# One excursion per pair of heads instead of two, the relu divided between two engines, and a new load order in a fused attention and feed-forward kernel

## The chip, the cores and the metric

The kernel runs on one core of a Trainium2 chip. The metric is the device time of the program in microseconds (us), the median of the runs. Runs of one kernel agree within about 0.3%. Profiled executions have a *span*, from the first to the last instruction, which is about 2 us shorter than the time. All numbers below are of one core; every profiled run that is compared had the state "fast".

Engines are named as in the profile: PE is the matmul engine (TensorE), PEld its weight loads, DVE is VectorE, ACT is ScalarE, POOL is GpSimd, SP the SyncE queue, which issues transposes by DMA and the output.

## The reference

Attention with a squared relu in place of softmax, then a feed-forward network with layer normalisation and a residual:

```python
scores = q @ k.T / sqrt(64)                      # q, k, v: 8 batches, 12 heads, 448 x 64
attn   = maximum(scores, 0)**2 / 448
x      = (attn @ v)  # heads side by side: 8 x 448 x 768
mu, var = mean(x), var(x)                        # over the 768
xn  = (x - mu) / sqrt(var + 1e-6) * g
out = x + maximum(xn @ w1, 0) @ w2               # w1: 768 x 3072, w2: 3072 x 768
```

Inputs and output are fp32; the kernel multiplies in bf16.

## The kernel before

The work is cut into 48 pairs of heads (8 batches, 6 pairs each). A pair has four score tiles; each is two matmuls of 64 rows (one per head) into one *score slot*, of which there are two. A relu and a square make the attention tile from it, and eight matmuls of 64 columns multiply it by v ("AV", one pair later).

```python
ps_sc = tile_pool(name="ps_sc", bufs=2, space=PSUM)   # two score slots
ps_f  = tile_pool(name="ps_f",  bufs=2, space=PSUM)   # feed-forward outputs
ps_m  = tile_pool(name="ps_m",  bufs=2, space=PSUM)   # AV, means, transposes

def att_QK(i, t):
    at = attn_pool.tile([SP, 2, S], bf16, tag="attn")
    sc = ps_sc.tile([P, 2, 512], fp32, tag="sc")
    for hh in range(2):
        nc.tensor.matmul(sc[:SP, hh, :S], ...)         # L209, 64 rows of the array
    nc.scalar.activation(at, sc[:SP, :, :S], Act.Relu) # L211, ScalarE reads the slot
    nc.vector.tensor_mul(at, at, at)                   # L212, square

def step_a(i): att_QK(i, 0); att_QK(i, 1)
def step_b(i):
    att_QK(i, 2); att_QK(i, 3); att_AV(i - 1)
    if ...: att_T(i + 3)                    # DMA transpose of q, k on the SP queue
```

The feed-forward matmuls use the whole array: `ps` blocks of 6 matmuls of 448 columns (first layer, L290) and `o_ps` blocks of 24 matmuls of 384 columns (second layer, L306). Between parts of such blocks the kernel pulls in the steps of the list above. I call each leaving of the full-array matmuls for the 64-row and 64-column ones an *excursion*. There are two per pair: 4 score matmuls, and 4 score plus 8 AV matmuls.

The feed-forward network runs for two batches at a time: first layer of one batch, first layer of the other, second layer of both. During the first layer of the second batch six DMA transposes (`ffn_x`, SP queue) turn x into rows, and DVE takes the statistics of these rows, which the output needs:

```python
if bb == 1 and ni < K1:
    items.append((0.0, lambda u=u, ki=ni: ffn_x(u, ki)))
if bb == 1 and ni >= K2 - MU:                                # from block 17 of 24
    items.append((0.0, lambda u=u, m=ni - (K2 - MU): ffn_stats(u, m)))
```

Batches 0 and 1 (pairs 0 to 11) have their q and k transposed on PE; from batch 2 (pair 12) on, the SP queue transposes them by DMA. Loads with a cast stand on one queue, and batch 2 stands behind w2:

```python
for c in range(W2C):       # W2C = 4
    load_w2(c)
load_paired(2)
```

Of the kernel before, what the change touches and what calls it, by code (L numbers as in the profile page):

```python
# [11 lines left out]
def kernel(  # L12
# [10 lines left out]
    nc = tc.nc  # L23
    P = 128
# [16 lines left out]
    U = 2  # L41
    UT = U * S
    MU = UT // P
    assert SP * NJ == S and MU * P == UT
    c2 = (1.0 / D) / S

# [38 lines left out]
    def alloc_batch(b):  # L85
        v_sb = v_pool.tile([SP, H, NJ * D], bf16, tag="v_sb")
        if b == 1:
            half = h1[:SP, :, S:S + NJ * D]
            qkv[b] = (half[:, :H, :], half[:, H:2 * H, :], v_sb)
            return  # L90
        q_sb = io_pool.tile([SP, H, NJ * D], bf16, tag="q_sb")
        k_sb = io_pool.tile([SP, H, NJ * D], bf16, tag="k_sb")
        qkv[b] = (q_sb, k_sb, v_sb)
# [19 lines left out]
                    by_pair[:, a, :, x, :],  # L113
                    src[b, 2 * a + x].rearrange("(p j) d -> p j d", j=NJ))

    def load_paired(b):
        alloc_batch(b)
        for a in range(NPAIR):
            load_pair(b, a)
            if a == 1:  # L120
                load_heads(b, [("v", 0, H)])
# [78 lines left out]
        qkT[i] = qkT_t  # L200
        nc.vector.tensor_copy(qkT[i], tp[0])  # L201

    def att_QK(i, t):
        at = attn_pool.tile([SP, 2, S], bf16, tag="attn")
        attn[i, t] = at
        sc = ps_sc.tile([P, 2, 512], fp32, tag="sc")
        for hh in range(2):
            r = slice(hh * D, (hh + 1) * D)
            nc.tensor.matmul(sc[:SP, hh, :S], qkT[i][r, 1, t * SP:(t + 1) * SP], qkT[i][r, 0, :],  # L209
                             start=True, stop=True)  # L210
        nc.scalar.activation(at, sc[:SP, :, :S], Act.Relu)  # L211
        nc.vector.tensor_mul(at, at, at)  # L212

    av = {}
    xs = {}
# [1 line left out]
    def xT_of(b, ki):  # L217
        return xT[b // U][:, ki, (b % U) * S:(b % U + 1) * S]

    def att_AV(i, half=None):  # L220
        b, pr = divmod(i, NPAIR)
        v_sb = qkv[b][2]
        if pr == 0 and half != 1:
            if b % U == 0:
                xT_t = xT_pool.tile([P, K1, UT], bf16, tag="xT")
                xT[b // U] = xT_t
            xs_t = xs_pool.tile([P, S], bf16, tag="xs")
            xs[b] = xs_t
        if half != 1:
            av_ps = ps_m.tile([P, S], fp32, tag="m")  # L230
            av[0] = av_ps
        ps = av[0]
        for t in range(NJ) if half is None else range(half * 2, half * 2 + 2):
            for hh in range(2):
                nc.tensor.matmul(  # L235
                    ps[hh * D:(hh + 1) * D, :],
                    v_sb[:, 2 * pr + hh, t * D:(t + 1) * D],
                    attn[i, t][:, hh, :],
                    start=(t == 0), stop=(t == NJ - 1))
        if half == 0:  # L240
            return
        nc.vector.tensor_scalar(xT_of(b, pr), ps, c2, None, op0=Alu.mult)  # L242
        if pr == 1:
            nc.vector.tensor_add(xs[b], xT_of(b, 0), xT_of(b, 1))
        elif 1 < pr < NPAIR - 1:
            nc.vector.tensor_add(xs[b], xs[b], xT_of(b, pr))  # L246

    xc = {}

    def center(b):  # L250
        mean_ps = ps_m.tile([P, S], fp32, tag="m")
        nc.tensor.matmul(mean_ps, ones, xs[b], start=True, stop=False)  # L252
        nc.tensor.matmul(mean_ps, ones, xT_of(b, K1 - 1), start=False, stop=True)  # L253
        xc_t = xc_pool.tile([P, K1, S], bf16, tag="xc")
        xc[b] = xc_t
        for ki in range(K1):
            nc.vector.tensor_sub(xc_t[:, ki, :], xT_of(b, ki), mean_ps)  # L257
# [38 lines left out]
    def ffn_2(u, m, j, part, parts):  # L296
        hd = d_model // 2
        if part == 0:
            if j == 0:
                o_t = o_pool.tile([P, d_model], fp32, tag="o")  # L300
                o_sb[0] = o_t
            o_ps = ps_f.tile([P, hd], fp32, tag="f")
            o_sb[1] = o_ps
        n = K2 // parts
        for ki in range(part * n, (part + 1) * n):
            nc.tensor.matmul(o_sb[1], h1[:, ki, m * P:(m + 1) * P], w2[:, ki, j * hd:(j + 1) * hd],  # L306
                             start=(ki == 0), stop=(ki == K2 - 1))
        if part == parts - 1:
            nc.vector.scalar_tensor_tensor(  # L309
                o_sb[0][:, j * hd:(j + 1) * hd], o_sb[1], rstd[u][:, m:m + 1],  # L310
                x_tok[u][:, m, j * hd:(j + 1) * hd], op0=Alu.mult, op1=Alu.add)
            if j == 1:
                c0 = m * P
                while c0 < (m + 1) * P:
                    g0 = c0 // SP
                    c1 = min((m + 1) * P, (g0 + 1) * SP)
                    bb, jj = divmod(g0, NJ)
                    nc.sync.dma_start(
                        out_tok[u * U + bb, c0 - g0 * SP:c1 - g0 * SP, jj, :],
                        o_sb[0][c0 - m * P:c1 - m * P, :])  # L320
                    c0 = c1


    def warm_up(n):
        w_ps = ps_f.tile([P, 256], fp32, tag="f")
        for _ in range(n):
            nc.tensor.matmul(w_ps, ones, warm, start=True, stop=True)  # L327
# [5 lines left out]
    def step_a(i):  # L333
        att_QK(i, 0)
        att_QK(i, 1)

    def step_b(i):
        att_QK(i, 2)
        att_QK(i, 3)
        if i > 0:  # L340
            att_AV(i - 1)
        if i + 2 < PE_T * NPAIR:
            att_T(i + 2)
        if PE_T * NPAIR <= i + 3 < NP_ALL:
            att_T(i + 3)
        b, r = divmod(i + 4, NPAIR)
        if r == 0 and PE_T < b < B:
            load_paired(b)

    def step_fine(i):  # L350
        att_QK(i, 0)
        if 0 < i < NPAIR - 1:
            att_T(i + 1)
        elif i > 0:
            warm_up(4)
        att_QK(i, 1)
        if i == 0:
            att_T(1)
            warm_up(1)
        else:  # L360
            att_AV(i - 1, 0)
        att_QK(i, 2)
        if i == 0:
            warm_up(4)
        else:
            att_AV(i - 1, 1)
        att_QK(i, 3)
        warm_up(4)

    def first_end():  # L370
        att_AV(NPAIR - 1, 0)
        att_T(NPAIR, evac=False)
        warm_up(4)
        att_AV(NPAIR - 1, 1)
        warm_up(8)
        center(0)
        att_T_out(NPAIR)

    for i in range(NP_ALL):
        if i < NPAIR:  # L380
            att.append(lambda i=i: step_fine(i))
        elif i == NPAIR:
            att.append(first_end)
            done_at.append(len(att))
            att.append(lambda i=i: (step_a(i), att_T(i + 1)))
            att.append(lambda i=i: (att_QK(i, 2), att_QK(i, 3), att_T(i + 2)))
        else:
            att.append(lambda i=i: step_a(i))
            att.append(lambda i=i: step_b(i))
            if i % NPAIR == 0:  # L390
                att.append(lambda b=i // NPAIR - 1: center(b))
                done_at.append(len(att))
# [4 lines left out]
    def steps_of(b):  # L397
        return done_at[b]

    NU = B // U  # L400
    segs = []
    CPN = K2 // NCH
    for u in range(NU):
        for bb in range(U):
            items = []
            for ni in range(K2):
                if bb == 0 and u == 0 and ni % CPN == 0 and ni // CPN + 1 < NCH:
                    c = ni // CPN + 1
                    items.append((0.0, lambda c=c: prep_w1(c, nc.vector, K1 // 2 if c < 3 else 0, K1)))
                if bb == 1 and ni < K1:  # L410
                    items.append((0.0, lambda u=u, ki=ni: ffn_x(u, ki)))
                if bb == 1 and ni >= K2 - MU:
                    items.append((0.0, lambda u=u, m=ni - (K2 - MU): ffn_stats(u, m)))
                items.append((1.12, lambda u=u, bb=bb, ni=ni: ffn_1(u, bb, ni)))
            segs.append((u * U + bb, items))
        items = []
        for m in range(MU):
            for j in range(2):
                for part in range(4):
                    items.append((0.96, lambda u=u, m=m, j=j, p=part: ffn_2(u, m, j, p, 4)))  # L420
                    if m + j + part == 0:
                        items.append((0.0, lambda u=u: ffn_stats(u, MU)))
        segs.append((u * U + U - 1, items))
# [6 lines left out]
    def pull():  # L430
        nonlocal ai
        att[ai]()
        ai += 1

    with tc.manual_schedule(engines=set(ENGINES)):
# [15 lines left out]
        warm_up(5)  # L451
        while ai < steps_of(0):
            pull()
        for c in range(W2C):
            load_w2(c)
        load_paired(2)

        pace = [(0.0, steps_of(0))]
        t = 0.0
# [51 lines left out]
```

## Time and profile before

| | before |
|---|---|
| time, median (lowest to highest) | 585.82 us (585.38 to 586.06) |
| span of the profiled run | 583.8 us |
| PE busy | 563.6 us, 97% |
| longest wait of PE | 8.93 us, at 72.5 us |

The page of the kernel before: the busy time of PE and ACT and DVE, then PE in 40 slices of the span (tenths), then the granted clock.

```profile
PE 563.6 (97%) x3542; PEld 287.3 (49%) x3542; DVE 263.6 (45%) x505; ACT 266.7 (46%) x392; POOL 143.3 (25%) x188
...
PE   8989949999999999999999999999999999999996
...
PEclk9999969999999999999999999999999999999999
```

PE is busy for 80% or more of every slice but the sixth (73 to 88 us) and the last, and in the sixth the clock falls too. That slice in the timeline of PE of the kernel before (start, duration, line, operation, shapes, count; in brackets the idle time before it and its releaser), and then one ordinary pair of excursions:

```profile
71.16 1.31 PE L290 MATMUL ps<-xc_t,w_112 128*128 128x448 bf16 x6
81.40 1.00 PE L209 MATMUL sc<-qkT_t 64*112 64x448 bf16 x4 [8.93 <-DMA qkT_t<-k_sb]
...
299.61 0.59 PE L209 MATMUL sc<-qkT_t 64*112 64x448 bf16 x4
300.13 0.95 PE L235 MATMUL av_ps<-at,v_sb 112*64 112x448 bf16 x8
301.01 4.07 PE L306 MATMUL o_ps<-w_113,h_114 128*128 128x384 bf16 x24
305.01 0.59 PE L209 MATMUL sc<-qkT_t 64*112 64x448 bf16 x4
305.53 5.05 PE L306 MATMUL o_ps<-w_113,h_114 128*128 128x384 bf16 x30
```

First reading: at 72.47 us PE stops for 8.93 us, because the transposed q and k of pair 12 are not there. Second reading, from starts: an excursion with AV takes 301.01 - 299.61 = 1.40 us, one without 0.52 us, a block of 24 matmuls 4.00 us. PE does not wait in either excursion.

Why pair 12 is late, in the timeline of the SP queue of the kernel before (the issue of transposes; the duration is the issue, not the landing):

```profile
72.27 1.29 SPq L177 DMA_TRANSPOSE qkT_t<-q_sb  x1
...
88.57 7.79 SPq L267 DMA_TRANSPOSE x_t<-xT_t  x5
...
101.60 1.25 SPq L267 DMA_TRANSPOSE x_t<-xT_t  x1
```

The transpose of pair 12 could be issued at 72.27 us only, when q had arrived behind w2. The first five transposes of x were issued from 88.57 us and the sixth at 101.60 us. In this kernel the first statistics came at 117.34 us.

What the stop did to the clock, in the windows of the kernel before (stretch, length, busy time of the engines; the value after POOL is the granted clock):

```profile
72.50:76.00 3.50, 0.00 (x0) 0.00 (x0) 1.11 (x3) 0.54 (x1) 3.50 (x6) 1.00 1.07 97
76.00:81.40 5.40, 0.00 (x0) 0.00 (x0) 0.00 (x0) 0.00 (x0) 2.30 (x4) 0.50 1.49 167
81.40:86.20 4.80, 4.80 (x18) 1.61 (x20) 1.25 (x2) 3.12 (x4) 3.94 (x6) 0.50 2.31 145
```

The clock fell to one half 3.5 us after the stop, and came back 4.8 us after PE resumed, at 86.2 us. The work in those 4.8 us cost about 2.2 us more than elsewhere. The Trainium skill ("TensorE: Matmul & The Clock Gate", Part 1) describes this: half clock after an idle window of about 3.4 us, full clock after a sustained busy one. The trace agrees for this fall (3.5 us). The windows also show a step: this stretch at half clock lasted 10.24 us (75.97 to 86.21 us), which is three times 3.41 us. With the 8.93 us of the stop the hole cost some 11.1 us.

Last, three groups of instructions of the kernel before (line, engine, operation, out and in, shapes, count, then busy us and mean ns of one, then idle time ahead):

```profile
L211 ACT ACTIVATE at<-sc 112x896 bf16<-112x896 f32 x192 | 165.0, 915 | 138.1 <-PE sc L209 137.6
...
L212 DVE TENSOR_TENSOR at<-at 112x896 bf16<-112x896 bf16 x192 | 120.2, 632 | 184.2 <-ACT at L211 184.2
...
L242 DVE TENSOR_SCALAR xT_t<-av_ps 128x448 bf16<-128x448 f32 x48 | 29.6, 617 | 3.6 <-PE av_ps L235 3.6
```

All relus are on ScalarE, 915 ns each; VectorE does the squares. The third line is how fast VectorE reads fp32 from PSUM: 617 ns for 448 columns.

### The profile page before, as it was taken

The page shows a single profiled execution, that of the slowest core. Times are in us where ns is not written, and L with a number is a line of the kernel's source. Part 1 is how long each engine was busy: PE and PEld are TensorE (multiplying, and loading weights), DVE is VectorE, ACT ScalarE, POOL GpSimd, SP SyncE. Part 2 cuts the span into 40 slices and gives each one's busy share as a digit, 9 for nine tenths or more (in the row PEclk, how much of TensorE's full clock was granted, in tenths as well). Part 3 has the DMA queues.
Part 4 walks back from the last instruction along what each step waited for, and adds up shares of the span by engine and source line. Part 5 has one row for each costly group of instructions (what it writes and reads, how often), then busy time and mean ns, then how long its engine had stood idle before and what let it go on. Part 6 is the DMA issues. An engine that isn't in the chain of part 4 may idle for free.

```text
span 583.8 us, 8969 instructions
## 1 busy us (share of the span) xinstructions
PE 563.6 (97%) x3542; PEld 287.3 (49%) x3542; DVE 263.6 (45%) x505; ACT 266.7 (46%) x392; POOL 143.3 (25%) x188
## 2 busy tenths in 40 slices
PE   8989949999999999999999999999999999999996
PEld 5444414445555444445555544445555544556663
DVE  4977814284544334375444424256454334401111
ACT  6937825672233576663232475664313364440000
POOL 7793170163006500074003610074000000000000
PEclk9999969999999999999999999999999999999999
DMA  9999999299218933599125954299223141000121
GB/s 181 201 205 210 195 145 129 38 116 96 71 44 105 154 36 58 78 111 104 44 71 66 169 54 80 47 95 112 54 58 73 47 71 33 0 2 28 55 54 55
DMA packets 153242, 51.79 MB, mean 89 GB/s; under 512 B 125808, under 2 KB 149616, under 8 KB 153200
## 3 DMA queue, kind: packets, MB, share of 16 engines
q0 software_dynamic: 90144, 25.50, 45.3%
q1 hardware_dynamic: 62576, 25.25, 22.0%
q8 instruction: 28, 0.46, 0.3%
q10 hardware_dynamic: 480, 0.46, 0.3%
q14 instruction: 14, 0.11, 0.1%
HBM read 51.91 MB, written 11.01 MB: 108 GB/s over the span
## 4 chain that ended last, share of the span: by engine, by line
PE 90%; DVE 5%; DMA 2%; ACT 1%; issue 0%; SPq 0%; ACTq 0%
PE o_ps L306 38%; PE ps L290 37%; PE sc L209 7%; PE av_ps L235 6%; DVE at L212 2%; ACT at L211 1%; DMA qkT_t<-k_sb 1%; DVE xc_t L257 1%; DMA h_114<-in_q_dram 1%; DVE qkT_t L201 1%; DVE xT_t L242 0%; DVE xs_t L246 0%; PE tp_ps L190 0%; PE mean_ps L253 0%; PE mean_ps L252 0%
## 5 line engine op out<-in xcount | busy, mean ns | idle before, releaser
L290 PE MATMUL ps<-xc_t,w_112 128*128 128x448 bf16 x1152 | 230.1, 354 | 1.8 <-DVE xc_t L257 1.8
L211 ACT ACTIVATE at<-sc 112x896 bf16<-112x896 f32 x192 | 165.0, 915 | 138.1 <-PE sc L209 137.6
L306 PE MATMUL o_ps<-w_113,h_114 128*128 128x384 bf16 x1344 | 225.6, 326 | 0.0
L212 DVE TENSOR_TENSOR at<-at 112x896 bf16<-112x896 bf16 x192 | 120.2, 632 | 184.2 <-ACT at L211 184.2
L306 PEld LDWEIGHTS <-h_114 128*128 128x128 bf16 x1344 | 128.6, 98 | 95.0 <-issue 12.2
L290 PEld LDWEIGHTS <-w_112 128*128 128x128 bf16 x1152 | 108.7, 98 | 115.6 <-issue 18.8
L292 ACT ACTIVATE h_114<-ps 128x448 bf16<-128x448 f32 x192 | 104.6, 545 | 110.6 <-PE ps L290 110.3
L112 POOL DMA_DIRECT2D q_sb<-in_q_dram x72 | 50.3, 703 | 213.1 <-DMA qkT_t<-q_sb 114.8
L309 DVE SCALAR_TENSOR_TENSOR o_t<-o_ps,rstd_t,x_t 128x384 f32<-128x384 f32 x56 | 34.5, 616 | 82.1 <-PE o_ps L306 82.1
L209 PE MATMUL sc<-qkT_t 64*112 64x448 bf16 x384 | 59.8, 378 | 10.3 <-DMA qkT_t<-k_sb 8.9
L112 POOL DMA_DIRECT2D k_sb<-in_k_dram x72 | 50.2, 701 | 38.8 <-DMA v_sb<-in_v_dram 26.2
L235 PE MATMUL av_ps<-at,v_sb 112*64 112x448 bf16 x384 | 47.3, 361 | 1.0 <-DVE at L212 0.6
L209 PEld LDWEIGHTS <-qkT_t 64*112 64x112 bf16 x384 | 18.4, 126 | 46.4 <-issue 34.3
L257 DVE TENSOR_TENSOR xc_t<-xT_t,mean_ps 128x448 bf16<-128x448 bf16 x48 | 26.2, 614 | 16.2 <-PE mean_ps L253 16.2
L242 DVE TENSOR_SCALAR xT_t<-av_ps 128x448 bf16<-128x448 f32 x48 | 29.6, 617 | 3.6 <-PE av_ps L235 3.6
L235 PEld LDWEIGHTS <-v_sb 112*64 112x64 bf16 x384 | 17.6, 109 | 24.7 <-issue 18.3
L159 POOL TENSOR_SCALAR w_112<-w_112,g_sb 128x512 bf16<-128x512 bf16 x12 | 20.8, 1744 | 1.3 <-DMA w_112<-in_moe_w_ch_dram 1.3
L284 DVE BATCH_NORM_STATS2 stats<-x_t 128x6 f32<-128x384 bf16 x28 | 15.2, 542 | 0.0
L283 DVE BATCH_NORM_STATS2 stats<-x_t 128x6 f32<-128x384 bf16 x28 | 14.6, 523 | 0.0
L327 PE MATMUL w_ps<-w_113,ones 128*128 128x256 bf16 x70 | 11.4, 304 | 1.2 <-DVE w_113 L77 1.2
L279 DVE RECIPROCAL rstd_t<-rstd_t 128x7 f32<-128x7 f32 x4 | 0.8, 201 | 22.5 <-ACT rstd_t L278 22.5
L246 DVE TENSOR_TENSOR xs_t<-xs_t,xT_t 128x448 bf16<-128x448 bf16 x24 | 10.0, 416 | 0.8
(36 smaller groups left out, 81.0 us busy)
## 6 DMA issues: line engine op xcount, KB each, us to landing
v_sb<-in_v_dram POOLq DMA_DIRECT2D x7, 672.0 KB, 10.0
w_112<-in_moe_w_ch_dram POOLq DMA_DIRECT2D x6, 768.0 KB, 25.8
w_113<-in_moe_w_ch_dram POOLq DMA_DIRECT2D x4, 1152.0 KB, 19.1
q_sb<-in_q_dram POOLq DMA_DIRECT2D x72, 56.0 KB, 4.1
k_sb<-in_k_dram POOLq DMA_DIRECT2D x72, 56.0 KB, 4.1
out_dram<-o_t SPq DMA_DIRECT2D x8, 336.0 KB, 2.8
out_dram<-o_t SPq DMA_DIRECT2D x8, 288.0 KB, 2.6
out_dram<-o_t SPq DMA_DIRECT2D x8, 240.0 KB, 2.6
```

The lines of the kernel that those rows point to most:

```text
L112: nc.gpsimd.dma_start(by_pair[:, a, :, x, :], src[b, 2 * a + x].rearrange("(p j) d -> p j d", j=NJ))
L159: eng.tensor_scalar(w, w, g_sb[:, ki:ki + 1], None, op0=Alu.mult)
L209: nc.tensor.matmul(sc[:SP, hh, :S], qkT[i][r, 1, t * SP:(t + 1) * SP], qkT[i][r, 0, :], start=True, stop=True)
L211: nc.scalar.activation(at, sc[:SP, :, :S], Act.Relu)
L212: nc.vector.tensor_mul(at, at, at)
L235: nc.tensor.matmul(ps[hh * D:(hh + 1) * D, :], v_sb[:, 2 * pr + hh, t * D:(t + 1) * D], attn[i, t][:, hh, :], start=(t == 0), stop=(t == N ...
L242: nc.vector.tensor_scalar(xT_of(b, pr), ps, c2, None, op0=Alu.mult)
L257: nc.vector.tensor_sub(xc_t[:, ki, :], xT_of(b, ki), mean_ps)
L290: nc.tensor.matmul(ps, w1[:, ki, ni * P:(ni + 1) * P], xc[u * U + bb][:, ki, :], start=(ki == 0), stop=(ki == K1 - 1))
L292: nc.scalar.activation(h1[:, ni, bb * S:(bb + 1) * S], ps, Act.Relu)
L306: nc.tensor.matmul(o_sb[1], h1[:, ki, m * P:(m + 1) * P], w2[:, ki, j * hd:(j + 1) * hd], start=(ki == 0), stop=(ki == K2 - 1))
L309: nc.vector.scalar_tensor_tensor(o_sb[0][:, j * hd:(j + 1) * hd], o_sb[1], rstd[u][:, m:m + 1], x_tok[u][:, m, j * hd:(j + 1) * hd], op0=A ...
```

## The change

The intent: fewer changes between the full array and its parts. From batch 2 on a pair makes one excursion: two score slots, AV of the pair behind, two score slots. As slots three and four reuse slots one and two at once, the relus are divided between VectorE and ScalarE, so that the slots come free sooner; the four squares come after. Besides, the first two pairs of batch 2 are loaded ahead of w2, the statistics start at block 10 and take every second block, the mean of batch 0 is summed pair by pair on PE, and the last output tile is written in halves.

```diff
-    def load_paired(b):
-        alloc_batch(b)
-        for a in range(NPAIR):
+    def load_paired(b, a0=0, a1=NPAIR):
+        if a0 == 0:
+            alloc_batch(b)
+        for a in range(a0, a1):
...
-        nc.scalar.activation(at, sc[:SP, :, :S], Act.Relu)
-        nc.vector.tensor_mul(at, at, at)
+        if relu_by is nc.vector:
+            nc.vector.tensor_scalar(at, sc[:SP, :, :S], 0.0, None, op0=Alu.max)
+        else:
+            nc.scalar.activation(at, sc[:SP, :, :S], Act.Relu)
+        if relu_by is None:
+            att_square(i, t)
...
+    def step_one(i):
+        att_QK(i, 0, relu_by=nc.vector)
+        att_QK(i, 1, relu_by=nc.scalar)
+        att_AV(i - 1)
+        att_QK(i, 2, relu_by=nc.vector)
+        att_QK(i, 3, relu_by=nc.scalar)
+        for t in range(NJ):
+            att_square(i, t)
+        next_T(i)
...
-            att.append(lambda i=i: step_a(i))
-            att.append(lambda i=i: step_b(i))
+            if i < PE_T * NPAIR:
+                att.append(lambda i=i: step_a(i))
+                att.append(lambda i=i: step_b(i))
+            else:
+                att.append(lambda i=i: step_one(i))
...
-                if bb == 1 and ni >= K2 - MU:
-                    items.append((0.0, lambda u=u, m=ni - (K2 - MU): ffn_stats(u, m)))
+                m = (ni - (K2 - 2 * MU)) // 2
+                if bb == 1 and m >= 0 and ni % 2 == 0:
+                    items.append((0.0, lambda u=u, m=m: ffn_stats(u, m)))
...
+        load_paired(2, 0, 2)
         for c in range(W2C):
             load_w2(c)
-        load_paired(2)
+        load_paired(2, 2)
```

(`att_square` holds the square; `next_T`, the end of the old `step_b`, issues the transposes of pair i + 3.)

More of the change, by code (lines that the diff above doesn't have):

```diff
@@ L43 @@
     MU = UT // P
+    NU = B // U
     assert SP * NJ == S and MU * P == UT
@@ L201, in att_T_out, with att_QK @@
         nc.vector.tensor_copy(qkT[i], tp[0])
-    def att_QK(i, t):
+    def att_QK(i, t, relu_by=None):
         at = attn_pool.tile([SP, 2, S], bf16, tag="attn")
@@ L210, in att_QK, with att_square @@
                              start=True, stop=True)
-        nc.scalar.activation(at, sc[:SP, :, :S], Act.Relu)
-        nc.vector.tensor_mul(at, at, at)
+        if relu_by is nc.vector:
[4 more added lines that the diff above has]
+            att_square(i, t)
+    def att_square(i, t):
+        nc.vector.tensor_mul(attn[i, t], attn[i, t], attn[i, t])
     av = {}
@@ L226, in att_AV @@
                 xT[b // U] = xT_t
-            xs_t = xs_pool.tile([P, S], bf16, tag="xs")
-            xs[b] = xs_t
+            if b > 0:
+                xs_t = xs_pool.tile([P, S], bf16, tag="xs")
+                xs[b] = xs_t
         if half != 1:
@@ L242, in att_AV @@
         nc.vector.tensor_scalar(xT_of(b, pr), ps, c2, None, op0=Alu.mult)
+        if b == 0:
+            return
         if pr == 1:
@@ L248, with mean_part @@
     xc = {}
-    def center(b):
-        mean_ps = ps_m.tile([P, S], fp32, tag="m")
-        nc.tensor.matmul(mean_ps, ones, xs[b], start=True, stop=False)
+    mean0 = {}
+    def mean_part(ki):
+        if ki == 0:
+            mean0_ps = ps_f.tile([P, S], fp32, tag="f")
+            mean0[0] = mean0_ps
+        nc.tensor.matmul(mean0[0], ones, xT_of(0, ki), start=(ki == 0), stop=(ki == K1 - 1))
+    def center(b):
+        if b == 0:
+            mean_ps = mean0[0]
+        else:
+            mean_ps = ps_m.tile([P, S], fp32, tag="m")
+            nc.tensor.matmul(mean_ps, ones, xs[b], start=True, stop=False)
         nc.tensor.matmul(mean_ps, ones, xT_of(b, K1 - 1), start=False, stop=True)
@@ L311, in ffn_2 @@
                 x_tok[u][:, m, j * hd:(j + 1) * hd], op0=Alu.mult, op1=Alu.add)
-            if j == 1:
+            last = u == NU - 1 and m == MU - 1
+            if j == 1 or last:
+                d0, d1 = (j * hd, (j + 1) * hd) if last else (0, d_model)
                 c0 = m * P
@@ L318, in ffn_2 @@
                     nc.sync.dma_start(
-                        out_tok[u * U + bb, c0 - g0 * SP:c1 - g0 * SP, jj, :],
-                        o_sb[0][c0 - m * P:c1 - m * P, :])
+                        out_tok[u * U + bb, c0 - g0 * SP:c1 - g0 * SP, jj, d0:d1],
+                        o_sb[0][c0 - m * P:c1 - m * P, d0:d1])
                     c0 = c1
@@ L343, in step_b, with next_T @@
             att_T(i + 2)
+        next_T(i)
+    def next_T(i):
         if PE_T * NPAIR <= i + 3 < NP_ALL:
@@ L348, in step_b @@
             load_paired(b)
+    def step_one(i):
[6 more added lines that the diff above has]
+            att_square(i, t)
+        next_T(i)
     def step_fine(i):
@@ L367, in step_fine @@
         att_QK(i, 3)
-        warm_up(4)
+        if i > 1:
+            mean_part(i - 2)
+            warm_up(2)
+        else:
+            warm_up(4)
     def first_end():
@@ L372, in first_end @@
         att_T(NPAIR, evac=False)
-        warm_up(4)
+        mean_part(NPAIR - 2)
+        warm_up(2)
         att_AV(NPAIR - 1, 1)
@@ L387 @@
         else:
-            att.append(lambda i=i: step_a(i))
-            att.append(lambda i=i: step_b(i))
+            if i < PE_T * NPAIR:
+                att.append(lambda i=i: step_a(i))
+                att.append(lambda i=i: step_b(i))
+            else:
+                att.append(lambda i=i: step_one(i))
             if i % NPAIR == 0:
@@ L398, in steps_of @@
         return done_at[b]
-    NU = B // U
     segs = []
```

## The prediction

> **What bounds the kernel now.** TensorE: the page gives PE 563.6 of 583.8 us (97%), and the chain of waits lies 90% on PE. The table of waits shows one real hole: 8.93 us (72.5 to 81.4) for the DMA transpose of batch 2's first pair, whose loads sit behind four w2 loads on the same queue (its waits on w_113 last until 71.8). The granted clock then fell to 0.5: in the timeline the next two blocks take 3.28 and 2.09 us against 1.76 and 1.40 elsewhere. Together about 11.1 us.
>
> **What the change does, costed.**
>
> 1. *One excursion per pair.* The timeline of PE shows 24 full-array matmuls of 384 columns in 4.00 us and 30 in 4.98: 163 ns each plus about 0.09 us per block. The Trainium skill ("TensorEngine Tiling (Array Packing)", Key Properties) says a change of tiling mode drains the array; the trace agrees in kind. One block less for each of 36 pairs: -3.2 us.
>
> 2. *A wait for score slots.* There are two score buffers. Slot two now starts behind 4 score and 8 AV matmuls, 1.40 us after the excursion's start (299.61 to 301.01). The first score is readable at +0.44 us (when ScalarE starts today). VectorE took 617 ns for 448 fp32 columns of PSUM; the skill ("VectorE: DVE Perf Modes", Mode 2×_2P) says two-port reading is SBUF only, so 896 should take about 1.08 us (estimate: 617 less 150 fixed, doubled). It ends at 1.52, so TensorE waits about 0.18 us in 30 excursions. In five excursions of the first second-layer stage an output eviction (616 ns) stands just ahead on VectorE: about 0.4 us. Together +7 us. VectorE rises by about 75 us, ScalarE falls by 66; neither becomes the bound.
>
> 3. *Pairs 0, 1 and v of batch 2 before w2.* The hole goes, with its cold clock: -11 us.
>
> 4. *But statistics seven blocks earlier.* In the first two batches they now stand on VectorE ahead of the relu of pair 14, and need all six transposes of x. Those queue on SyncE behind the transposes of pairs 14 and 15, which still wait for loads behind w2. DMA is saturated from 40 to 90 us in both orders, so these loads should land near 82 us (83.3 before). Then 5 us of transposes, 8 of x (88.6 to 96.4 today), 2.6 for pair 16, the last x transpose and 2.9 to landing: about 101.5. Statistics and relu end near 103.6; TensorE would want slot two near 95.8. I expect a new hole of 4 to 8 us there, perhaps 2 us of cold clock: most of step 3 is given back.
>
> 5. Small: first mean without sums (-1), batch 1's mean subtracted late behind four squares (+0.8), last output in two pieces (-0.3).
>
> Sum, with the hole at the small end for doubt: 584 us, 577 to 590. Chances: faster 8%, within 2% 90%, slower 2%.
>
> **What would show it.** The hole at 72 us gone; a PE wait on VectorE's relu for the score tile in nearly every excursion, 5 to 9 us in total; one PE wait of 4 to 8 us near 96 to 104 us, with VectorE's statistics waiting on the x transposes; relu on VectorE near 1.08 us; blocks of 42 to 48 matmuls between excursions.
>
> **What would make it wrong.** If w2 loads run faster in the new order, or the x transposes land before about 95 us, hole 4 vanishes: near 577. If VectorE reads PSUM faster than estimated, step 2 vanishes and 5 to 7 us more go, giving over 2%. If VectorE falls behind in the stages with statistics (about 10.3 us of work in a 10.5 us period), step 2 grows.

## The result

| | before | after |
|---|---|---|
| time, median (lowest to highest), 4 runs each | 585.82 us (585.38 to 586.06) | 588.19 us (587.28 to 588.36) |
| span of the profiled run | 583.8 us | 586.2 us |
| DVE busy | 263.6 us | 325.1 us |
| ACT busy | 266.7 us | 213.1 us |

The ratio of the times is 1.0038, with a 95% interval of 1.0021 to 1.0056. A ratio here is the mean time of one kernel's fast runs over that of the other's of the same rounds, so it is not quite the ratio of the medians quoted. The prediction was 584.0, 577 to 590, most likely within 2%.

The page of the kernel after:

```profile
PE 564.6 (96%) x3536; PEld 295.0 (50%) x3536; DVE 325.1 (55%) x573; ACT 213.1 (36%) x320; POOL 144.0 (25%) x188
...
PE   8989995899999999999999999999999999999997
...
PEclk9989998799999999999999999999999999999999
```

The dip of PE has not gone; it has moved on by a slice, to 88 to 103 us, with the clock low in that slice and the next. The timeline of PE of the kernel after, around that place and for one excursion later on:

```profile
86.16 0.59 PE L211 MATMUL sc<-qkT_t 64*112 64x448 bf16 x4
...
87.74 0.59 PE L211 MATMUL sc<-qkT_t 64*112 64x448 bf16 x4
88.26 6.98 PE L313 MATMUL ps<-xc_t,w_112 128*128 128x448 bf16 x36
95.17 0.59 PE L211 MATMUL sc<-qkT_t 64*112 64x448 bf16 x4
95.69 0.95 PE L245 MATMUL av_ps<-at,v_sb 112*64 112x448 bf16 x8
104.18 0.99 PE L211 MATMUL sc<-qkT_t 64*112 64x448 bf16 x4 [7.54 <-DVE at L214]
```

In pair 13 (86.16 us) the third score starts 1.58 us after the first; in pair 14 (95.17 us) it starts 9.01 us after. The difference, 7.43 us, is a new hole, and its releaser is the relu on VectorE (L214). What VectorE did then, in its timeline of the kernel after:

```profile
96.05 0.56 DVE L306 BATCH_NORM_STATS2 stats<-x_t 128x6 f32<-128x384 bf16 x1 [4.63 <-DMA x_t<-xT_t]
102.37 0.56 DVE L307 BATCH_NORM_STATS2 stats<-x_t 128x6 f32<-128x384 bf16 x1 [5.75 <-DMA x_t<-xT_t]
...
103.09 1.04 DVE L214 TENSOR_SCALAR at<-sc 112x896 bf16<-112x896 f32 x1
```

VectorE waited 4.63 us for the first transposes of x and then 5.75 us for the sixth, and the relu of pair 14, which had its scores from about 95.6 us, stood behind these statistics. The Trainium skill ("TensorE: Matmul & The Clock Gate", "Architectural detail: the array is 16× 32×32, not 1× 128×128") says that the queues of ScalarE and VectorE are strictly first in, first out; the trace agrees, as a relu that was ready did not pass an instruction waiting 5.75 us. And the SP queue of the kernel after shows why the sixth transpose came then:

```profile
89.66 6.90 SPq L290 DMA_TRANSPOSE x_t<-xT_t  x5
...
99.31 1.25 SPq L290 DMA_TRANSPOSE x_t<-xT_t  x1
```

The transposes of x were still issued from 89.66 us (88.57 before), the sixth at 99.31 us (101.60 before): the first five stand behind those of pairs 14 and 15, whose loads stand behind w2 still, and the sixth also behind that of pair 16. But now their first user asks for them at 91 us instead of 117 us. The windows of the kernel after show the clock:

```profile
96.50:99.30 2.80, 0.14 (x2) 0.12 (x1) 0.11 (x1) 0.22 (x1) 0.00 (x0) 1.00 0.67 127
99.30:104.10 4.80, 0.00 (x0) 0.00 (x0) 1.70 (x4) 0.00 (x0) 0.00 (x0) 0.50 0.36 70
104.10:109.50 5.40, 5.32 (x16) 2.06 (x16) 5.33 (x12) 1.46 (x2) 1.28 (x2) 0.50 0.22 43
```

PE ran at half clock until 109.5 us. The two score matmul pairs took 0.92 us from start to start of the next block instead of 0.52, and the 42 matmuls after them 10.22 us instead of the 8.06 that 42 take elsewhere: 2.56 us more with the 0.40 of the scores. The hole cost about 10.0 us in all, against 11.1 of the old one.

The groups that answer to those of before:

```profile
L216 ACT ACTIVATE at<-sc 112x896 bf16<-112x896 f32 x120 | 106.9, 917 | 189.1 <-PE sc L211 189.0
...
L214 DVE TENSOR_SCALAR at<-sc 112x896 bf16<-112x896 f32 x72 | 78.2, 1086 | 88.7 <-PE sc L211 88.7
L221 DVE TENSOR_TENSOR at<-at 112x896 bf16<-112x896 bf16 x192 | 109.9, 623 | 11.3 <-ACT at L216 11.2
```

A relu of 896 columns from PSUM costs VectorE 1086 ns. The Trainium skill ("VectorE: DVE Perf Modes", Why PSUM operands drop a tier) says that reading through both ports needs SBUF, so fp32 in PSUM is read at the basic rate; 1086 against 617 ns for twice the columns agrees. If the time is a fixed part and a part for each column, the two durations give a fixed part of 2 × 617 - 1086 = 148 ns; the prediction had assumed 150.

Where did the steady part go? I added up the time from each block's start to the next one's, by kind, from the first to the last `o_ps` block of each trace:

| between the first and the last second-layer block | before | after |
|---|---|---|
| `o_ps` blocks | 167.43 us in 41 | 165.76 us in 24 |
| `ps` blocks | 166.54 us in 35 | 166.74 us in 20 |
| AV matmuls, 33 pairs | 29.04 us | 35.10 us |

Merging saved (167.43 - 165.76)/17 = 0.098 us per `o_ps` block that is no longer broken up. The `ps` blocks would have saved (166.54 - 166.74 + 1.38)/15 = 0.079 us each, 1.38 us being two new waits that are explained next. But AV and the gap behind it grew by 6.06/33 = 0.18 us per pair: that is the wait for a score slot, 1.58 instead of 1.40 us to the third score. (The table of waits does not list it, because the short gap of PE, 0.11 us behind the modelled end of the AV matmuls, is too small.) Per pair this is a loss of about 0.1 us.

One of the two new waits of PE, in the timeline of all engines of the kernel after (the other, at 470.24 us, is alike):

```profile
331.42 2.22 DVE L221 TENSOR_TENSOR at<-at 112x896 bf16<-112x896 bf16 x4
...
333.02 2.31 PE L313 MATMUL ps<-xc_t,w_112 128*128 128x448 bf16 x11 [0.69 <-ACT h_114 L315]
333.56 0.61 DVE L332 SCALAR_TENSOR_TENSOR o_t<-o_ps,rstd_t,x_t 128x384 f32<-128x384 f32 x1
```

The last second-layer output is evicted at 333.56 us only, behind four squares. It holds one of the two `ps_f` buffers meanwhile, so the new stage's second block waits for the other to be emptied. That reading rests on the order in the trace; no run was made to test it alone. The two waits, 1.3 to 1.4 us together, do stand in every trace with single excursions (after, e1, e2, e5, e7, e9, e10) and in none with two.

### The profile page after: what moved, and what is told of

The parts are those of the page before. It is cut to its first block, busy times and chain, and to the rows that moved or that the text cites. A ratio compares the mean times of both kernels' runs of the same rounds, so it can differ in the third digit from the quotient of the medians.

```text
span 586.2 us, 8903 instructions
## 1 busy us (share of the span) xinstructions
PE 564.6 (96%) x3536; PEld 295.0 (50%) x3536; DVE 325.1 (55%) x573; ACT 213.1 (36%) x320; POOL 144.0 (25%) x188
## 4 chain that ended last, share of the span: by engine, by line
PE 84%; DVE 9%; ACT 2%; SPq 2%; DMA 1%; issue 1%; ACTq 0%; DVEq 0%
PE o_ps L329 38%; PE ps L313 35%; PE sc L211 8%; DVE at L214 6%; ACT at L216 2%; PE av_ps L245 1%; SPq L290 1%; DVE at L221 1%; DVE xc_t L280 1%; DMA h_114<-in_q_dram 1%; PE tp_ps L192 1%; SPq L179 1%; PE w_ps L352 1%; DMA x_t<-xT_t 1%; DVE xT_t L252 0%
## 5 line engine op out<-in xcount | busy, mean ns | idle before, releaser
L329 PE MATMUL o_ps<-w_113,h_114 128*128 128x384 bf16 x1344 | 222.7, 326 | 0.0
L216 ACT ACTIVATE at<-sc 112x896 bf16<-112x896 f32 x120 | 106.9, 917 | 189.1 <-PE sc L211 189.0
L329 PEld LDWEIGHTS <-h_114 128*128 128x128 bf16 x1344 | 130.0, 98 | 90.5 <-issue 5.6
L313 PEld LDWEIGHTS <-w_112 128*128 128x128 bf16 x1152 | 111.0, 99 | 116.0 <-issue 18.0
L214 DVE TENSOR_SCALAR at<-sc 112x896 bf16<-112x896 f32 x72 | 78.2, 1086 | 88.7 <-PE sc L211 88.7
L221 DVE TENSOR_TENSOR at<-at 112x896 bf16<-112x896 bf16 x192 | 109.9, 623 | 11.3 <-ACT at L216 11.2
L113 POOL DMA_DIRECT2D k_sb<-in_k_dram x72 | 51.6, 719 | 35.6 <-DMA v_sb<-in_v_dram 20.0
L211 PEld LDWEIGHTS <-qkT_t 64*112 64x112 bf16 x384 | 22.9, 125 | 47.1 <-issue 41.6
L352 PE MATMUL w_ps<-w_113,ones 128*128 128x256 bf16 x60 | 11.1, 329 | 1.2 <-DVE w_113 L78 1.2
```

Source lines behind the costliest of these rows:

```text
L113: nc.gpsimd.dma_start(by_pair[:, a, :, x, :], src[b, 2 * a + x].rearrange("(p j) d -> p j d", j=NJ))
L211: nc.tensor.matmul(sc[:SP, hh, :S], qkT[i][r, 1, t * SP:(t + 1) * SP], qkT[i][r, 0, :], start=True, stop=True)
L214: nc.vector.tensor_scalar(at, sc[:SP, :, :S], 0.0, None, op0=Alu.max)
L221: nc.vector.tensor_mul(attn[i, t], attn[i, t], attn[i, t])
L313: nc.tensor.matmul(ps, w1[:, ki, ni * P:(ni + 1) * P], xc[u * U + bb][:, ki, :], start=(ki == 0), stop=(ki == K1 - 1))
L329: nc.tensor.matmul(o_sb[1], h1[:, ki, m * P:(m + 1) * P], w2[:, ki, j * hd:(j + 1) * hd], start=(ki == 0), stop=(ki == K2 - 1))
```

## The experiments

The theories, by the letters that I gave them. About the hole at 97 us: (A) VectorE's statistics wait for the transposes of x, and the relu stands behind them in the queue; (B) VectorE simply has too much to do in that stage; (C) DMA bandwidth, not the order of loads, sets when the x transposes land. About the 0.18 us of each excursion: (D) the third score waits for the slot, that is for the end of the relu; (F) it is the cost of changing the shape of the array on PE itself, drained once more in the middle of the excursion. All "times" are medians; ratios are against the kernel before on the same chip. Its median was 585.98 us beside the first four runs, 585.68 beside the next four, 585.74 beside the last three.

### Statistics late in the first stage (e1_stats_late)

```diff
-                m = (ni - (K2 - 2 * MU)) // 2
-                if bb == 1 and m >= 0 and ni % 2 == 0:
+                late = u == 0
+                m = ni - (K2 - MU) if late else (ni - (K2 - 2 * MU)) // 2
+                if bb == 1 and m >= 0 and (late or ni % 2 == 0):
```

> The changed kernel, but the statistics of the first two batches go back to their old place (the last seven blocks); everything else stays. Theory A (the hole of 7.5 us at 97 us is VectorE standing in order behind statistics that wait for the x transposes): hole and its cold clock (2.5 us more) go, 577 to 580 us, the excursion of pair 14 restarts its third score at +1.58 us like the others. Rival B (VectorE is simply overfull since it took half the relus): the same work packed into fewer blocks makes it no better, waits of several us reappear near 110 to 125 us, 584 us or more.

Measured: 580.54 us (579.74 to 582.42), ratio 0.9909 [0.9893, 0.9926], span 578.4. The hole is gone. The timeline of PE in this run, at pair 14 and at a later excursion:

```profile
93.97 0.58 PE L211 MATMUL sc<-qkT_t 64*112 64x448 bf16 x4
...
95.56 0.59 PE L211 MATMUL sc<-qkT_t 64*112 64x448 bf16 x4
...
117.64 0.40 PE L211 MATMUL sc<-qkT_t 64*112 64x448 bf16 x2 [1.53 <-DVE at L214]
```

The third score of pair 14 comes after 1.59 us, as in pair 13 of the changed kernel. So it was the place of the statistics (A). VectorE's load (B) is not nothing: at the old place, one per block, the statistics delay a relu by 1.53 us. After that stop the clock fell, in the windows of this run:

```profile
118.53:121.95 3.42, 3.42 (x13) 1.59 (x12) 3.26 (x7) 2.04 (x3) 2.81 (x5) 0.50 1.69 120
```

So the block of 48 at 117.97 us took 9.58 instead of 7.91 us: PE did not wait in it, it ran at half clock for 3.41 us. In the 3.41 us ahead of the fall (115.12 to 118.53 us) PE had still been busy for 1.75 us. The relu's delay and the clock together cost 3.2 us, more than the 0.5 us by which the median lay above the range I gave; how far they explain that, one trace does not show, since the mean clock of the other runs (0.994 to 1.0) differs.

### All of batch 2 ahead of w2 (e2_loads_all_first)

```diff
-        load_paired(2, 0, 2)
+        load_paired(2)
         for c in range(W2C):
             load_w2(c)
-        load_paired(2, 2)
```

> The changed kernel, but all six pairs of batch 2 are loaded before w2, not only two; the early statistics stay. Theory A: the transposes of pairs 14 and 15 no longer wait for loads behind w2, x transposes start near 73 us instead of 89.7 and land before 95, the hole goes, 577 to 580 us. Rival B (VectorE overfull): the statistics stay where they are, the hole stays, 587 to 589. Rival C (the DMA engines are full anyway, so the x transposes come late whatever the order): hole shrinks by half at most, 582 to 586.

Measured: 591.17 us (588.75 to 591.82), ratio 1.0077 [1.0058, 1.0097], span 589.3. My expectation failed: the hole grew. The SP queue of this run, then below VectorE's timeline of the same run:

```profile
77.72 22.59 SPq L290 DMA_TRANSPOSE x_t<-xT_t  x5
```

```profile
106.09 0.56 DVE L307 BATCH_NORM_STATS2 stats<-x_t 128x6 f32<-128x384 bf16 x1 [5.75 <-DMA x_t<-xT_t]
...
106.81 1.04 DVE L214 TENSOR_SCALAR at<-sc 112x896 bf16<-112x896 f32 x1
```

The transposes of x were indeed issued 12 us earlier (77.72 instead of 89.66 us). But five of them took 22.59 us instead of 6.90, since w2's loads now ran beside them: from 78 to 100 us the loading queue moved 3.02 MB and the transposing one 1.22 MB. The statistics again waited 5.75 us for the sixth, and PE 12.85 us for the relu. The mechanism (A) is seen a second time, in its last link. The remedy failed in the way of (C): with all of batch 2 ahead, the w2 loads ran beside the transposes of x and those were slow. That the loads made them slow is read from this traffic; no run tested it alone. The Trainium skill ("DMA: Bandwidth & Descriptors", Queues, rings and completion order) says that each DMA engine goes round between the queues that have work for it, a packet at a time. That fits two queues slowing each other, but I did not measure the turns.

### The old load order (e7_loads_old)

```diff
-        load_paired(2, 0, 2)
         for c in range(W2C):
             load_w2(c)
-        load_paired(2, 2)
+        load_paired(2)
```

> The changed kernel with the old load order (w2 ahead of all of batch 2). Theory A (a hole opens wherever VectorE reaches the statistics before the x transposes land near 102 us): the old hole of 9 us returns at 72 us, everything after it is 11 us later, so pair 14's excursion starts near 104 us and hardly waits; only one hole, 587 to 591 us, within 0.5% of the changed kernel. Rival (two independent holes): both stand, 597 to 600 us.

Measured: 589.33 us (587.92 to 589.92), ratio 1.0056 [1.0041, 1.0071], span 588.1. The timeline of PE in this run:

```profile
83.23 0.99 PE L211 MATMUL sc<-qkT_t 64*112 64x448 bf16 x4 [12.35 <-DMA qkT_t<-k_sb]
```

The hole of before is back, and the one at 97 us is gone: the wait at 83 us is 12.35 us, longer than the 8.93 of before. Pair 14 comes at 107.16 us only, when the x transposes have landed, and its third score comes after 1.59 us. So the first hole had been hiding the second. In the changed kernel the new load order is worth about 1 us net at most, because it trades one hole for the other; the intervals of the two ratios (1.0056 here, 1.0038 for the changed kernel) overlap, so even that is not clear of noise.

### The load order alone, in the kernel before (e8_loads_only)

```diff
+        load_paired(2, 0, 2)
         for c in range(W2C):
             load_w2(c)
-        load_paired(2)
+        load_paired(2, 2)
```

(with the two arguments of `load_paired` that this needs)

> The kernel before with the new load order alone. Theory A: the hole at 72 us and its cold clock go and nothing takes their place, since no relu stands on VectorE and the statistics are late: 574 to 576 us, 11 us less than before. If the small parts (first mean, last output in two pieces) are worth 2 to 3 us, the run with two excursions (572.3) is that much faster than this one. Rival (the order only moves the hole elsewhere): 582 or more.

Measured: 573.59 us (573.37 to 573.94), ratio 0.9790 [0.9777, 0.9804], span 571.8. With two excursions, relus on ScalarE and late statistics, the load order alone is worth 12 us (2.1%; the interval spans 2%). In the traces 11.1 us of it are the hole; another 1.1 us is an earlier first feed-forward block (33.09 instead of 34.23 us), in code that the edit does not touch. Nothing takes the hole's place: after the first microseconds no wait of PE in this run is longer than 0.8 us.

### Two excursions, everything else as after (e3_two_excursions)

```diff
-            if i < PE_T * NPAIR:
+            if i < NP_ALL:
                 att.append(lambda i=i: step_a(i))
                 att.append(lambda i=i: step_b(i))
```

> The changed kernel with two excursions per pair and all relus on ScalarE as before; loads, early statistics, mean and tail as changed. Theory A plus D (each single excursion pays 0.19 us for a score slot still being read and saves one block of 0.09 us): no relu stands on VectorE, so the late statistics hold nobody and the hole goes too: 588 less 10 less 35 times 0.10 = 574 to 576. Rival E (the single excursion is a gain of 3 us and only the hole spoils it): 580 to 582.

Measured: 572.31 us (571.84 to 573.93), ratio 0.9773 [0.9755, 0.9792], span 570.0: faster than both kernels. The timeline of PE of this run around the place of the hole:

```profile
95.33 0.59 PE L211 MATMUL sc<-qkT_t 64*112 64x448 bf16 x4
...
96.73 3.58 PE L313 MATMUL ps<-xc_t,w 128*128 128x448 bf16 x18
```

No hole here, though the statistics are as early as in the changed kernel and the transposes of x no sooner (the sixth issued at 99.30 us). VectorE even waits for it, in its timeline of this run:

```profile
103.97 0.56 DVE L307 BATCH_NORM_STATS2 stats<-x_t 128x6 f32<-128x384 bf16 x1 [7.46 <-DMA x_t<-xT_t]
```

What differs is that the relus are on ScalarE, so VectorE may wait 7.46 us while PE goes on. This shows which of the parts made the hole: neither the early statistics nor the relu on VectorE does it alone; both together do. The stages now take what they took before (67.71, 67.65, 67.70, 67.64 us from first block to first block), against 68.1 to 70.5 us in the changed kernel.

### Each relu divided between the engines by head (e5_split_relu)

```diff
-        if relu_by is nc.vector:
-            nc.vector.tensor_scalar(at, sc[:SP, :, :S], 0.0, None, op0=Alu.max)
+        if relu_by is not None:
+            nc.vector.tensor_scalar(at[:, 0, :], sc[:SP, 0, :S], 0.0, None, op0=Alu.max)
+            nc.scalar.activation(at[:, 1, :], sc[:SP, 1, :S], Act.Relu)
```

> The changed kernel, but each relu of a single excursion is split: head 0 on VectorE, head 1 on ScalarE, at once, so that the first score slot is free near +1.06 us (second layer) or +1.25 us (first layer, where ScalarE first has a hidden relu) instead of +1.53. The hole at 97 us stays. Theory D (the third score waits for the slot's reader): third score at +1.40 to +1.43 us in place of +1.58; the fourth may wait up to 0.2 us in the first layer; 582 to 586 us. Rival F (the extra 0.18 us is the drain from AV back to score tiling, not a reader): +1.58 stays, 588 us.

Measured: 606.22 us (605.25 to 606.87), ratio 1.0343 [1.0325, 1.0361], span 605.0. The run did not do what I meant it to. Both halves write one tile, and the second half was made to wait for the first, by a semaphore of the program: ACT's half ran after DVE's (its releaser in the trace is "DVE at L214"), so the slot was free later, not sooner. From the fourth single excursion on, the third score came after 1.75 to 1.95 us and the excursion took 2.61 to 2.81. As a test of a quick release it is void. Still, the third score moved with the end of its reader, while PE's own work was the same, which speaks for (D) against (F).

### A relu that reads half (e9_half_read)

```diff
-            nc.vector.tensor_scalar(at, sc[:SP, :, :S], 0.0, None, op0=Alu.max)
+            nc.vector.tensor_scalar(at[:, :, :S // 2], sc[:SP, :, :S // 2], 0.0, None, op0=Alu.max)
+            nc.vector.tensor_copy(at[:, :, S // 2:], at[:, :, :S // 2])
+        elif relu_by is nc.scalar:
+            nc.scalar.activation(at[:, :, :S // 2], sc[:SP, :, :S // 2], Act.Relu)
+            nc.scalar.activation(at[:, :, S // 2:], at[:, :, :S // 2], Act.Relu)
```

> Wrong result on purpose: in single excursions each relu reads only half of the score columns and copies that half into the rest of its own tile, so the slot is free after about 0.6 us of reading, while the work on all engines stays about as long. Theory D (the third score waits for the reader of its slot): third score at +1.40 us after the excursion's start instead of +1.58, excursion 1.92 us instead of 2.10; the hole at 97 us stays; 581 to 583 us. Rival F (a drain on the way back from AV to score tiling costs the 0.18 us): +1.58 stays, 588.

The result is wrong (relative error 0.67): half of the scores are dropped, so that the slot is free after a shorter read while PE's work stays the same. Measured: 581.19 us (580.74 to 581.90), ratio 0.9920 [0.9907, 0.9933], span 580.1. The timeline of PE of this run:

```profile
345.20 0.59 PE L211 MATMUL sc<-qkT_t 64*112 64x448 bf16 x4
...
346.60 0.59 PE L211 MATMUL sc<-qkT_t 64*112 64x448 bf16 x4
347.11 2.06 PE L317 MATMUL ps<-xc_t,w 128*128 128x448 bf16 x10
```

The third score comes after 1.40 us and the excursion takes 1.91 us, against 1.58 and 2.10: the 0.18 us was the slot (D), not PE (F). The hole stayed (10.8 us), as A wants. This is also the bound of the idea: without the wait the second-layer stages take 67.07 us against 67.70 with two excursions, some 0.1 us per pair, or about 3.6 us over 36 pairs. A correct version that frees the slot so early I did not find: halves in separate tiles might let both engines read at once, but no run tried them.

### All four relus on ScalarE in the single excursion (e10_relu_scalar)

```diff
-        att_QK(i, 0, relu_by=nc.vector)
+        att_QK(i, 0, relu_by=nc.scalar)
         att_QK(i, 1, relu_by=nc.scalar)
         att_AV(i - 1)
-        att_QK(i, 2, relu_by=nc.vector)
+        att_QK(i, 2, relu_by=nc.scalar)
```

> The changed kernel with all four relus of a single excursion on ScalarE. Theory A: no relu behind the statistics, so no hole at 97 us (10 us less). Theory D: the second slot is read after the first (0.86 us each), so the fourth score waits until about +2.35 us (second layer) or +2.5 us (first layer, behind a hidden relu), 0.75 to 0.9 us more per excursion than in the changed kernel, 27 to 32 us in all: 603 to 610 us. If the excursion's extra time were a drain and not a reader, it would be 578.

Measured: 597.70 us (595.48 to 598.78), ratio 1.0193 [1.0172, 1.0214], span 593.7. The hole at 97 us is gone, as it needs VectorE's relu. A smaller one remains: at 105.08 us the AV matmuls wait 1.28 us in all for squares that VectorE did late, behind the same statistics. The timeline of PE of this run:

```profile
351.89 0.40 PE L211 MATMUL sc<-qkT_t 64*112 64x448 bf16 x2
352.70 0.40 PE L211 MATMUL sc<-qkT_t 64*112 64x448 bf16 x2 [0.41 <-ACT at L216]
```

Now the fourth score waits for the second relu in a row, and an excursion takes 2.54 us in the second layer and 2.70 in the first. I had expected a larger loss; the second relu ends about 0.86 us after the first, so the wait added 0.4 to 0.6 us per pair and not 0.75 to 0.9. The mechanism held, its size did not. It also shows that dividing the relus between the engines was the right choice for a single excursion: 2.10 us against 2.54 to 2.70.

### Which of the fast versions, on one chip (e11_two_exc, e12_loads, e13_two_exc_stats_old)

The two best had run on different chips. The third pair of runs repeats them on one: the first is the code of e3_two_excursions, the second that of e8_loads_only. The third is the first with this edit:

```diff
-                m = (ni - (K2 - 2 * MU)) // 2
-                if bb == 1 and m >= 0 and ni % 2 == 0:
+                m = ni - (K2 - MU)
+                if bb == 1 and m >= 0:
```

> The two-excursion version with everything else of the change, once more, to stand on one chip beside the load order alone: 572.3 if chips agree. If the small parts (mean by pieces, last output in two pieces) are worth something, it is 1.0 to 1.7 us under the load order alone, as start and tail in the two traces say (first FFN matmul 31.93 against 33.09, last stage to end 59.0 against 59.7); if the difference of before (572.31 against 573.59 on two chips) was the chips, the two agree within 0.5.

Measured: 572.39 us (571.72 to 574.59), ratio 0.9775 [0.9756, 0.9794].

> The load order alone, on the same chip as the two-excursion version: 573.4 to 573.9 if the small parts are worth 1.0 to 1.7 us, 572.3 plus or minus 0.5 if they are worth nothing.

Measured: 573.97 us (573.84 to 575.42), ratio 0.9802 [0.9789, 0.9816].

> The two-excursion version with the statistics of all batch pairs at their old place. The first-to-first gaps of the stages are the same to 0.1 us in the two-excursion version (early statistics) and in the load order alone (late ones), so the early statistics should be worth nothing: within 0.5 us of the two-excursion version. If late statistics cost an eviction at the start of each second-layer stage, as in the run with late statistics in the single-excursion kernel (1.67 us in its first stage), it is 1 to 3 us slower.

Measured: 572.20 us (571.62 to 573.63), ratio 0.9770 [0.9756, 0.9784].

The medians of the first two differ by 1.6 us, the size that start and tail in the traces give, but the intervals of their ratios overlap (0.9789 to 0.9794), so the order of these two is likely and not certain. The early statistics show no gain: 572.20 without them, 572.39 with them. They only made sense as room for VectorE's relus, which they then blocked. So the best version is: two excursions, the new load order, the mean by pieces and the last output in halves, 2.3% faster than before.

## Why the prediction was right, and where it was not

The time, 588.19 us, lay within the range and within 2%, as said. The mechanisms were those predicted. The sizes were not all, and the forecast of 584 was 4.2 us too low.

- **The hole at 72 us goes: -11.** Right; it is gone from the trace. Run alone, the load order gave 12 us (e8).
- **One block less for each of 36 pairs: -3.2.** About right: 0.098 and 0.079 us per block, near 3 us for 36.
- **Slot wait of 0.18 us in 30 excursions.** Right: third score at 1.58 us in place of 1.40, and e9 shows it to be the slot. The relu's 1.08 us was measured as 1.086.
- **0.4 us in the five excursions with an eviction ahead.** Wrong: 0.20 us (third score at +1.60). In the first of them (144.35 us) VectorE's relu ran from 144.99 to 146.07 us, but the third score began at 145.94: it used the slot that ScalarE, at 144.97 us, had been given, and the fourth took the other. I had tied the third score to VectorE's slot. It cost only 1 us in the sum.
- **A new hole of 4 to 8 us with perhaps 2 us of cold clock, by statistics that wait for x transposes.** Right in cause and place: e1, e3, e7 and e10 each remove it by removing one link. My own chain gave the relu's end as 103.6 us (measured: 104.13) and the time at which PE wants slot two as 95.8 us, which is a hole near 7.8 us; it measured 7.43 us, with 2.56 us of cold clock. The step that failed is the last one, "Sum, with the hole at the small end for doubt: 584". Taking the chain at its word would have given about 588. That this would have met the time so closely is partly luck: the waits and the clock dip of the next two points, 2.75 us, were not foreseen, and the start, the tail and batch 1's mean came out better than forecast by 2.2 us.
- **Not foreseen:** the two waits of 0.69 us behind the squares, 1.4 us.
- **Small terms.** Between the two profiled runs the start saved 2.0 us (first FFN block at 32.20 instead of 34.23 us), not 1; but e8 and e12, which have the start of the kernel before, reach that block at 33.09 and 33.24 us, and against these the saving is the 1 us forecast. The profiled run then had half clock from 34.4 to 37.9 us, about 1.35 us, which other runs with the same start did not have. The tail saved 0.7, not 0.3. Batch 1's mean cost no 0.8 us: its late subtractions were hidden by 17 first-layer matmuls still to be done, with 0.18 us of wait (0.15 before).
- **VectorE +75, ScalarE -66.** Measured +61.5 and -53.6 us; I had left out that fewer sums are made and that the busy time of the squares falls (120.2 to 109.9 us). The relus on ScalarE lost only 58.1 us of busy time (165.0 to 106.9). Neither is a bound, so it did not matter.

The terms added up: -2.0 (start) + 1.35 (clock dip) - 11.1 (old hole) + 10.0 (new hole) + 6.7 (slot, 36 times 0.185) - 3.0 (blocks) + 1.4 (two waits) - 0.7 (tail) = +2.65 us, against +2.4 us of span.

So the change did what it was meant to do, fewer blocks, and this was worth 3 us; it paid 6.7 us for it at the slots. Its real gain, the load order, was hidden: moving relus to VectorE tied PE to an engine whose queue held an instruction waiting for a late DMA. What stays open: a correct single excursion with earlier free slots, and what exactly made the clock dip by 1.35 us near 35 us, in the traces of this run and of e12 and in no other. A lead: in the 3.41 us ahead of the fall (31.03 to 34.44 us) PE, waiting for VectorE, was busy for 1.97 us, and in e12 for 1.99 us; in the other traces no such step between 25 and 40 us had less than 2.15 us. No run tested this, and the share of busy time alone is not the rule: near the end of e7, 1.42 us in such a step left the clock up.

## What to carry to other kernels

Before moving work onto an engine on the critical path's behalf, list what stands in that engine's queue at that time and what each of these instructions waits for: an engine with 45% of the time free can still hold up PE for 7 us. When one large wait is removed, look for the next late thing behind it, since the first hole may have hidden a second; run each part of a change by itself, as the best version here is the change without its headline. When a chain of times gives a hole, put its value in the sum, and put doubt in the range.

## What the Trainium skill lacked or had wrong

- "TensorEngine Tiling (Array Packing)", Key Properties, says that a change of tiling mode drains the array, without a size. Here joining two full-array blocks saved 0.098 us (384 columns) and 0.079 us (448 columns) per block. This includes whatever else a block's start and end cost.
- "TensorE: Matmul & The Clock Gate", Part 1, gives the return to full clock as about 4 us after sustained work begins, give or take 0.5. Here it came 4.8 us and 5.3 us after PE resumed. The fall came 3.5 and 2.7 us after the stop, where the page gives an idle window of about 3.4; and no whole idle window was needed: in the 3.41 us ahead of the fall PE was busy for 0.76 us (changed kernel, 95.88 to 99.29 us), 1.75 us (e1) and 1.97 us (changed kernel, 31.03 to 34.44 us).
- "DMA: Bandwidth & Descriptors" has the turn-taking of queues but no cost for transposes beside casting loads: five DMA transposes of x took 6.90 us, and 22.59 us beside the loads of w2.
- No page that I read warns of what e5 met: two engines were given halves of one tile, and a semaphore of the program made the second wait for the first, so that the third score came after 1.75 us instead of 1.58. This is how the program was built and not shown to be a limit of the chip.
